# Storing the cache gradients of a decode step's backward pass from ScalarE, one head later, with the last two heads in parts

## The chip, the cores and the metric

The kernel runs on one core of a Trainium2 chip. The metric is the device time of one launch in microseconds, taken as the median of several runs. Times inside the kernel come from one profiled execution.

## The reference

The reference computes one decode step of a transformer layer (batch 4, one token each, D = 512, 32 heads of 128, a key and a value cache of 4096 positions per head) and its gradients for a given `grad_out`, all in bf16:

```
xn = layernorm(x);  q = xn @ wq                       # per batch b and head h: q of 128
p  = softmax(q . K^T / sqrt(128));  o = p @ V         # K, V: [4, 32, 4096, 128]
h  = x + concat(o) @ wo
h2 = h + (silu(hn @ w1) * (hn @ w3)) @ w2,  hn = layernorm(h)
outputs: h2, and the gradients of x, k_cache, v_cache, wq, wo, w1, w3, w2
```

The large part is the caches. There are 4 x 32 = 128 heads, and each has 1 MB of keys and 1 MB of values. For one head with output gradient dO (128 values) the backward pass is

```
dP = V @ dO                     # 4096 values
dS = p * (dP - c) * scale       # c = dO . o
grad of V = p  (outer) dO       # 4096 x 128, out_3
grad of K = dS (outer) q        # 4096 x 128, out_2
```

So keys and values are read once for the forward pass (256 MB), the values are read a second time for dP (128 MB), and 256 MB of outer products are written.

## The kernel before, in words

The order of all work is written out by hand; every engine executes its instructions in program order. All large tiles live in 22 equal buffers in SBUF, called slots. A slot is taken from the front of one queue (`free`) and given back at its end (`give`), at the place in the program where the last use is written; the next user of the slot waits for that last use, for instance until a store from it has landed.

The forward part (until about 690 us of the trace) loads K and V head by head on SP's DMA queue and computes the softmax and, per head, a 128 x 128 product. A middle part (690 to 720 us) does the gated unit and its gradients. The backward loop over the 128 heads `s` then follows, from 720 us on; `b, h = s % B, s // B`. In one iteration:

- `prefetch(s + 1)` issues loads of V on SP's queue, up to seven heads ahead and as long as more than five slots are free.
- `front(s + 1)` transposes that head's V on TensorE in four groups of eight blocks (L739), ScalarE copies each group from PSUM to the slot VT (L740), TensorE multiplies VT by dO (L1070, dP), and GpSimd writes the pairs of p (L1073). Every fourth head, `replicate` makes the broadcast rows `rq` and `rdo` (L1054 on TensorE, L1057 on ScalarE).
- `back(s)` makes the two outer products on VectorE (both at L1077): first gv, the gradient of V, then dS (L1092, L1095), then gk, the gradient of K. After each of them GpSimd issued the store of the 1 MB (L1089, L1099), and the slot was given back there.
- `step("s", n)` lets `n` pieces of the side work run: the gradients of x, wq, wo, w1, w3, w2, which use TensorE, ScalarE and slots of their own, and whose stores GpSimd issues (gwq, gw, gwo). It runs one piece per head for 44 heads and then two, with a third on every fourth head.

After the loop the rest of the side work would run; in this kernel it has ended by then.

At the start of the loop most slots are taken: eight by the forward products (Ms, given back during the first 48 heads), ten by loaded V, one by `rs`.

Of the kernel before, what the change touches and what calls it, by code (L numbers as in the profile page):

```python
# [24 lines left out]
def kernel(  # L25
# [22 lines left out]
    nc = tc.nc  # L48
    P = nc.NUM_PARTITIONS

    B = A_x.shape[0]
    D = A_x.shape[-1]
    H = A_k_cache.shape[1]
# [30 lines left out]
    def bh_of(s):  # L84
        return s % B, s // B

    def rows_of(ap):
        return ap.rearrange("(p j) d -> p j d", p=P)
# [83 lines left out]
    def ones_window(col):  # L172
# [11 lines left out]
                          in_=rowg[:, None, :, None].to_broadcast([P, 4, 8, 4]))  # L184
# [414 lines left out]
    def step(k, n=1):  # L599
        for _ in range(n):  # L600
            next(units[k], None)
# [131 lines left out]
    def V_T(s, ps):  # L733
        VTs[s] = Slot("VT")
        VT, Vn = VTs[s].heads(), V2s[s].heads()
        for g in range(SJ // GW):
            pt = ps.tile([P, GW, P], BF16, tag="tps", name="pt_tps")
            for i in range(GW):
                nc.tensor.transpose(pt[:, i, :], Vn[:, g * GW + i, :], ident_b[:])  # L739
            nc.scalar.copy(out=VT[:, g * GW:(g + 1) * GW, :], in_=pt[:])  # L740
        V2s.pop(s).give()
# [3 lines left out]
    def load_V2():  # L745
        s = nv["next"]
        if s < NH:
            V2s[s] = Slot("V2")
            nc.sync.dma_start(out=V2s[s].heads(), in_=cache_head(A_v_cache, s))
            nv["next"] += 1  # L750
# [125 lines left out]
    with ExitStack() as c2:  # L876
# [173 lines left out]
        def replicate(i0):  # L1050
            for nm_, rows in (("rdo", dOrows_bf), ("rq", qrows_bf)):
                ps = psrep.tile([P, REP, Dh], FP32, tag="rep", name="rep_ps")
                for i in range(REP):
                    nc.tensor.matmul(ps[:, i, :], lhsT=ident_b[:, i0 + i:i0 + i + 1].to_broadcast([P, P]), rhs=rows[:],  # L1054
                                     start=True, stop=True)
                rt = rep_bufs[nm_][i0 // REP % 2]
                nc.scalar.copy(out=rt, in_=ps[:])  # L1057
                reps[nm_, i0 // REP] = rt
# [3 lines left out]
        def front(s):  # L1062
            if s % REP == 0:
                replicate(s)
            if s not in VTs:
                V_T(s, psT)
            VT = VTs[s].heads()
            dP_ps = psD.tile([P, SJ], FP32, name="dP_ps", tag="dP")
            for j in range(SJ):
                nc.tensor.matmul(dP_ps[:, j:j + 1], lhsT=VT[:, j, :], rhs=dOT_bf[:, s:s + 1], start=True, stop=True)  # L1070
            VTs.pop(s).give()
            P2 = bw3.tile([P, SJ, 2], BF16, tag="P2", name="P2")
            nc.gpsimd.tensor_copy(out=P2[:], in_=P_all[:, s, :, None].to_broadcast([P, SJ, 2]))  # L1073
            bwd[s] = (dP_ps, P2)

        def outer(dst, col2, row):
            nc.vector.tensor_tensor(  # L1077
                out=dst.rearrange("p j (r t) -> p j r t", t=2),
                in0=col2[:, :, None, :].to_broadcast([P, SJ, Dh // 2, 2]),
                in1=row.rearrange("p (r t) -> p r t", t=2)[:, None, :, :].to_broadcast([P, SJ, Dh // 2, 2]),  # L1080
                op=ALU.mult,
            )

        def back(s):
            b, h = bh_of(s)
            dP_ps, P2 = bwd.pop(s)
            gv = Slot("gv")
            outer(gv.heads(), P2, reps["rdo", s // REP][:, s % REP, :])
            nc.gpsimd.dma_start(out=rows_of(out_3[b, h]), in_=gv.heads())  # L1089
            gv.give()  # L1090
            t = bw3.tile([P, SJ], FP32, tag="dSt", name="dSt")
            nc.vector.tensor_scalar(out=t[:], in0=dP_ps[:], scalar1=c_rep[:, s:s + 1], scalar2=scale,  # L1092
                                    op0=ALU.subtract, op1=ALU.mult)
            dS2 = bw3.tile([P, SJ, 2], BF16, tag="dS2", name="dS2")
            nc.vector.tensor_tensor(out=dS2[:], in0=t[:, :, None].to_broadcast([P, SJ, 2]),  # L1095
                                    in1=P_all[:, s, :, None].to_broadcast([P, SJ, 2]), op=ALU.mult)
            gk = Slot("gk")
            outer(gk.heads(), dS2, reps["rq", s // REP][:, s % REP, :])
            nc.gpsimd.dma_start(out=rows_of(out_2[b, h]), in_=gk.heads())  # L1099
            gk.give()  # L1100

        def prefetch(s):
            while nv["next"] < min(NH, s + 7) and len(free) > 5:
                load_V2()

        prefetch(0)
        front(0)
        for s in range(NH):
            prefetch(s + 1)
            if s + 1 < NH:  # L1110
                if s + 1 not in V2s and s + 1 not in VTs:
                    load_V2()
                front(s + 1)
            back(s)
            step("s", 1 if s < 44 else 2 + (s % 4 == 0))
        step("s", 400)


# [28 lines left out]
```

## Time and profile before

| what | value |
|---|---|
| median of 8 runs | 1742.61 us (1740.53 to 1749.5) |
| the profiled execution | 1749.5 us, span 1747.7 us |
| DMA | 707.86 MB, mean 405 GB/s |
| busy share | PE 75%, DVE 72%, ACT 55%, POOL 28% |
| one outer product on VectorE | 2.29 us, 256 of them |
| one copy of eight transposed blocks on ScalarE | 1.015 us, 512 of them |
| issue of one store on GpSimd | 0.53 us, 256 of them; median to landing 20 us |
| first and last store of the loop | issued at 722.0 and 1727.5 us |

In the lines of the profile PE is TensorE (PEld its weight loads), DVE is VectorE, ACT is ScalarE, POOL is GpSimd and SP is SyncE, whose queue issues the loads. `out<-in` names the tile that an instruction writes and the one that it reads. A row of waits reads: engine, its instruction, what it waited for; total us, how often, longest. A row of windows gives the busy time and the number of instructions of each engine, then the granted TensorE clock, the mean busy share of the 16 DMA engines, and their rate in GB/s.

### The profile page before, as it was taken

To read this page: it belongs to the slowest core of one execution; us is meant where nothing else is said; L and a number is where in the kernel's file an instruction comes from. 1 tells how busy PE (TensorE), PEld (TensorE's weight loads), DVE (VectorE), ACT (ScalarE), POOL (GpSimd) and SP (SyncE) were. 2 spreads that over 40 slices of the span, in tenths; PEclk is the share of its full clock that TensorE was granted. 3 is DMA by queue.
4 is the path that set the end of the run, shared out by engine and by line. 5 is a ranking of instruction groups with operands and counts; after the bars stand their busy time and mean duration, and the time that the engine had idled before them with its cause. 6 is when DMAs were issued, how large, how long until landed. Compare 5 with 4: busy or idle time off the path is not lost.

```text
span 1747.7 us, 44065 instructions
## 1 busy us (share of the span) xinstructions
PE 1316.4 (75%) x18993; PEld 1112.7 (64%) x18993; DVE 1251.6 (72%) x1382; ACT 955.6 (55%) x1463; POOL 483.4 (28%) x804
## 2 busy tenths in 40 slices
PE   5889888888888888888777876676667657786653
PEld 4777776666666667877767875565445545564543
DVE  5899899899898996567756866648545546665665
ACT  3455445445444444656555665575556656676643
POOL 2333333333333330122322421212212112222232
PEclk8999999999999999655555557676556655556565
DMA  9999999999999999799999999999999999999997
GB/s 398 410 418 418 419 418 419 419 416 418 413 417 394 418 404 359 304 421 411 418 419 419 415 418 414 420 423 375 422 383 405 411 400 411 391 411 415 405 421 313
DMA packets 107123, 707.86 MB, mean 405 GB/s; under 512 B 11232, under 2 KB 18920, under 8 KB 23984
## 3 DMA queue, kind: packets, MB, share of 16 engines
q1 hardware_dynamic: 67280, 422.68, 59.4%
q0 software_dynamic: 39648, 282.36, 39.2%
q8 instruction: 149, 2.44, 0.5%
q14 instruction: 46, 0.38, 0.1%
HBM read 422.58 MB, written 282.34 MB: 403 GB/s over the span
## 4 chain that ended last, share of the span: by engine, by line
DMA 32%; PE 9%; DVE 9%; ACT 7%; issue 6%; POOL 1%; DVEq 0%; POOLq 0%; ACTq 0%
DMA out_dram<-gk 21%; DMA out_dram<-gv 8%; ACT VT L740 6%; DVE gk L1077 4%; PE pt_tps L739 3%; DVE gv L1077 3%; DMA out_dram<-gwo 2%; PE dq_ps L902 2%; DMA out_dram<-gw 1%; PE dP_ps L1070 1%; PE M_ps L436 1%; DVE PK L421 1%; PE pt_wo L573 1%; POOL P L1073 0%; PE rep_ps L1054 0%
## 5 line engine op out<-in xcount | busy, mean ns | idle before, releaser
L740 ACT COPY VT<-pt_tps 128x1024 bf16<-128x1024 bf16 x512 | 492.7, 1015 | 292.2 <-PE pt_tps L739 141.9
L739 PE MATMUL pt_tps<-ident_b,V 128*128 128x128 bf16 x4096 | 446.5, 291 | 179.0 <-ACT VT L740 171.3
L739 PEld LDWEIGHTS <-V 128*128 128x128 bf16 x4096 | 396.7, 137 | 246.4 <-issue 228.6
L1077 DVE TENSOR_TENSOR gv<-P,reps 128x4096 bf16<-128x4096 bf16 x128 | 292.9, 2288 | 254.2 <-DMA out_dram<-gk 145.1
L1077 DVE TENSOR_TENSOR gk<-dS,reps 128x4096 bf16<-128x4096 bf16 x128 | 293.4, 2292 | 79.0 <-DMA out_dram<-gk 32.6
L421 DVE TENSOR_TENSOR PK<-Kn,PK 128x4096 bf16<-128x4096 bf16 x128 | 302.8, 2366 | 37.3 <-POOL PK L417 37.3
L436 PE MATMUL M_ps<-PK,Vn 128*128 128x130 bf16 x4096 | 287.5, 223 | 53.7 <-DMA Vn<-in_A_v_cache_dram 53.6
L436 PEld LDWEIGHTS <-Vn 128*128 128x128 bf16 x4096 | 254.3, 99 | 74.3 <-DMA Vn<-in_A_v_cache_dram 66.9
L328 DVE STREAM_TRANSPOSE KT<-Kn 128x512 f32<-128x512 f32 (+1 forms) x321 | 250.8, 798 | 0.5 <-issue 0.5
L323 ACT COPY KT<-pt_tps 128x1024 bf16<-128x1024 bf16 x128 | 129.4, 1012 | 194.1 <-PE pt_tps L322 161.4
L1070 PE MATMUL dP_ps<-dOT_bf,VT 128*128 128x1 bf16 x4096 | 152.7, 166 | 75.8 <-ACT VT L740 64.4
L1070 PEld LDWEIGHTS <-VT 128*128 128x128 bf16 x4096 | 140.8, 104 | 89.0 <-ACT VT L740 76.9
L1099 POOL DMA_DIRECT2D out_dram<-gk x128 | 68.2, 532 | 392.3 <-DVE gk L1077 376.5
L1089 POOL DMA_DIRECT2D out_dram<-gv x128 | 68.5, 535 | 354.3 <-DVE dSt L1092 337.4
L417 POOL COPY PK<-P_all 128x64 bf16<-128x64 bf16 x128 | 32.3, 252 | 437.7 <-ACT P_all L411 432.5
L336 POOL COPY zq<-qT_bf 128x2 bf16<-128x2 bf16 x128 | 152.2, 1189 | 0.0
L1073 POOL COPY P<-P_all 128x64 bf16<-128x64 bf16 x128 | 114.1, 892 | 0.0
L411 ACT COPY P_all<-pt_P 32x64 bf16<-32x64 bf16 x256 | 51.9, 203 | 59.7 <-PE pt_P L407 57.4
L322 PE MATMUL pt_tps<-ident_b,Kn 128*128 128x128 bf16 x1024 | 80.0, 222 | 0.7 <-DVE qrep L282 0.7
L446 PE MATMUL kP_ps<-PK,onesw 128*32 128x512 bf16 x1024 | 80.1, 390 | 0.0
L322 PEld LDWEIGHTS <-Kn 128*128 128x128 bf16 x1024 | 61.6, 99 | 26.3 <-issue 26.2
L400 ACT ACTIVATE Pn<-E,rl 128x1024 bf16<-128x1024 f32 x64 | 73.7, 1152 | 2.8 <-DVE rl L397 2.8
(234 smaller groups left out, 1301.2 us busy)
## 6 DMA issues: line engine op xcount, KB each, us to landing
Kn<-in_A_k_cache_dram SPq DMA_DIRECT2D x128, 1024.0 KB, 14.8
Vn<-in_A_v_cache_dram SPq DMA_DIRECT2D x128, 1024.0 KB, 15.5
V<-in_A_v_cache_dram SPq DMA_DIRECT2D x128, 1024.0 KB, 11.7
out_dram<-gv POOLq DMA_DIRECT2D x128, 1024.0 KB, 20.1
out_dram<-gk POOLq DMA_DIRECT2D x128, 1024.0 KB, 20.3
wq<-in_A_wq_dram SPq DMA_DIRECT2D x8, 1024.0 KB, 11.2
out_dram<-gw POOLq DMA_DIRECT2D x6, 896.0 KB, 21.6
wo<-in_A_wo_dram SPq DMA_DIRECT2D x4, 1024.0 KB, 11.7
```

Source lines behind the costliest of these rows:

```text
L322: nc.tensor.transpose(pt[:, i, :], Kn[:, c * GW + i, :], ident_b[:])
L323: nc.scalar.copy(out=KT[:, c * GW:(c + 1) * GW, :], in_=pt[:])
L328: nc.vector.transpose(out=KT[:, c * w_:(c + n) * w_], in_=Kn[:, c * w_:(c + n) * w_])
L336: nc.gpsimd.tensor_copy(out=zq[gi % 2][hl][:, 32:132:67], in_=qT_bf[:, s:s + 1].to_broadcast([P, 2]))
L421: nc.vector.tensor_tensor(out=PK[:, :, 0:Dh].rearrange("p j (r t) -> p j r t", t=2), in0=Ks[s].heads().rearrange("p j (r t) -> p j r t", t=2),
L436: nc.tensor.matmul(hold["M"][:], lhsT=Vn[:, j, :], rhs=PK[:, j, :], start=(j == 0), stop=(j == SJ - 1))
L446: nc.tensor.matmul(hold["kP"][32 * q:32 * (q + 1), :, :], lhsT=ones_window(w), rhs=PK[:, j0:j0 + 4, 0:Dh], start=(w == 0 and c == 0), stop ...
L739: nc.tensor.transpose(pt[:, i, :], Vn[:, g * GW + i, :], ident_b[:])
L740: nc.scalar.copy(out=VT[:, g * GW:(g + 1) * GW, :], in_=pt[:])
L1070: nc.tensor.matmul(dP_ps[:, j:j + 1], lhsT=VT[:, j, :], rhs=dOT_bf[:, s:s + 1], start=True, stop=True)
L1073: nc.gpsimd.tensor_copy(out=P2[:], in_=P_all[:, s, :, None].to_broadcast([P, SJ, 2]))
L1077: nc.vector.tensor_tensor(out=dst.rearrange("p j (r t) -> p j r t", t=2), in0=col2[:, :, None, :].to_broadcast([P, SJ, Dh // 2, 2]), in1=r ...
```

## The change

The stores of a head are taken out of `back(s)`. `back` appends the two slots to a queue `late`, and a new function `store_late(eng)` issues the two stores of the oldest entry on the engine that it is given and gives the slots back. In the loop it is called with ScalarE between `front(s + 1)` and `back(s)`, so the stores of head s stand in ScalarE's queue after the copies of head s + 2. Heads 0 and 1 are stored by GpSimd right after their `back`. For the last head of the two last batches (h = 31, b = 2 and 3, which are s = 126 and 127) each store is cut into one of 120 partitions and one of 8. The last entry is stored after the loop, before the rest of the side work. The side work gets its third piece on every third head instead of every fourth. The side work's own stores stay on GpSimd.

```
 def back(s):
     ...
     outer(gv.heads(), P2, reps["rdo", s // REP][:, s % REP, :])
-    nc.gpsimd.dma_start(out=rows_of(out_3[b, h]), in_=gv.heads())
-    gv.give()
     ...
     outer(gk.heads(), dS2, reps["rq", s // REP][:, s % REP, :])
-    nc.gpsimd.dma_start(out=rows_of(out_2[b, h]), in_=gk.heads())
-    gk.give()
+    late.append((b, h, gv, gk))
+
+late = deque()
+
+def store_late(eng):
+    b, h, gv, gk = late.popleft()
+    for out_ap, sl in ((out_3, gv), (out_2, gk)):
+        cut = [0, 120, P] if h == H - 1 and b >= B - 2 else [0, P]
+        for p0, p1 in zip(cut[:-1], cut[1:]):
+            eng.dma_start(out=rows_of(out_ap[b, h])[p0:p1], in_=sl.heads()[p0:p1])
+        sl.give()
 ...
+S0 = 0
 prefetch(0)
 front(0)
 for s in range(NH):
     ...
         front(s + 1)
+    if late:
+        store_late(nc.scalar)
     back(s)
-    step("s", 1 if s < 44 else 2 + (s % 4 == 0))
+    if s < 2:
+        store_late(nc.gpsimd)
+    if s >= S0:
+        step("s", 1 if s < S0 + 44 else 2 + (s % 3 == 0))
+store_late(nc.scalar)
 step("s", 400)
```

## The prediction

> **What bounds the kernel now.** I read the 40 slices first, then the queues and the issues, then the stages by window, then the waits, and last the timeline of both ends of the backward part.
>
> ```profile
> DMA  9999999999999999799999999999999999999997
> GB/s 398 410 418 418 419 418 419 419 416 418 413 417 394 418 404 359 304 421 411 418 419 419 415 418 414 420 423 375 422 383 405 411 400 411 391 411 415 405 421 313
> q1 hardware_dynamic: 67280, 422.68, 59.4%
> q0 software_dynamic: 39648, 282.36, 39.2%
> V<-in_A_v_cache_dram SPq DMA_DIRECT2D x128, 1024.0 KB, 11.7
> out_dram<-gv POOLq DMA_DIRECT2D x128, 1024.0 KB, 20.1
> out_dram<-gk POOLq DMA_DIRECT2D x128, 1024.0 KB, 20.3
> ```
>
> The 16 DMA engines are busy in every slice but the middle one (17) and the last. 707.86 MB are moved and the change moves no byte more or less, so it can only change idle DMA time, the speed of a packet, and what follows the last byte. A V load lands in 11.7 us, a store in 20: stores queue.
>
> ```profile
> core 0: us, PE busy (x) PEld busy (x) DVE busy (x) ACT busy (x) POOL busy (x), PEclk, DMA share, GB/s
> 720.00:740.00 20.00, 16.98 (x224) 15.91 (x223) 14.33 (x12) 13.53 (x15) 5.17 (x9) 0.59 0.63 233
> 740.00:752.00 12.00, 10.03 (x135) 9.33 (x134) 5.64 (x5) 7.19 (x9) 1.40 (x4) 0.62 1.00 394
> 752.00:1180.00 428.00, 326.93 (x4116) 298.54 (x4114) 275.96 (x227) 249.76 (x272) 113.26 (x166) 0.59 1.01 418
> 1180.00:1660.00 480.00, 324.71 (x3960) 258.46 (x3956) 289.10 (x241) 299.37 (x375) 116.00 (x187) 0.59 0.99 403
> 1732.00:1736.00 4.00, 0.00 (x0) 0.00 (x0) 0.00 (x0) 0.00 (x0) 0.00 (x0) 0.50 0.87 367
> 1736.00:1740.00 4.00, 0.00 (x0) 0.00 (x0) 0.00 (x0) 0.00 (x0) 0.00 (x0) 0.50 0.21 90
> 1740.00:1744.00 4.00, 0.00 (x0) 0.00 (x0) 0.00 (x0) 0.00 (x0) 0.00 (x0) 0.50 0.06 25
> ```
>
> The last two columns matter. The backward loop starts with a DMA that is not full (0.63), is full from 740 on, loses rate after 1180 (403 against 418), and ends with a tail in which few engines still write: a share of 0.06 is one engine of 16. ScalarE is busy 250 of 428 us and 299 of 480: it has room for more issues.
>
> ```profile
> DVE gv L1077 <- DMA out_dram<-gk: 145.1, 37, 9.8
> ACT VT L740 <- DMA out_dram<-gv: 49.2, 12, 8.8
> ACT VT L740 <- DMA out_dram<-gk: 48.8, 11, 11.6
> ```
>
> The waits of the backward loop say the same: the products and the V^T copies wait until a store has landed and its slot is free.
>
> **One finding behind the page.** A transfer's semaphore counts 16 engines. In the trace's semaphore events the 16th engine of a store comes 0.4 us after the 15th between 740 and 900 us (median), 6.5 us after it between 1200 and 1650, 3.1 us after it for the very last store (1740.8, then 1743.9); for loads before 660 us it is 0.1 us. Packets follow one another on an engine within 3 to 4 ns, so the packet records can be put into 16 chains: between 1700 and 1716 eight or nine chains write 8 KB in 309 ns each, without exception, and four or five take 314 to 321 ns on the mean. So some engines are slower than the rest, only while GpSimd's queue is in use, and a slot waits for the slowest. On one point the measured queue numbers are no help: packets of both queues cost the same (39.2% for 282 MB, 59.4% for 423 MB).
>
> **The change, part by part.** The profiled execution took 1749.5 us (1.8 around its span of 1747.7); the median of the runs is 1742.6. The terms below are differences and I put them on the median. 0.2%, about what a measurement of this kernel can tell from no change, is 3.5 us: 1739.1 to 1746.1.
>
> *Who issues.* 252 stores of 1 MB leave GpSimd (0.53 us each, idle there anyway) for ScalarE. The trace has no ScalarE store. The nearest rows are SP's loads: 0.33 us alone, 1.1 to 1.6 us each when several follow one another in the backward loop. Two per head make 0.7 to 3 us; between two heads ScalarE idles 1.34 to 2.6 us for TensorE's first eight transposes (timeline), which is the cover. Taken at +1 us in all, 0 to +8.
>
> *Slow engines.* If the slow chains come from GpSimd's way of issuing, they go. Time of 8 KB packets over 309 ns is 2.05% of the engines in 740 to 1180 (9 us) and 3.4% in 1180 to 1660 (16 us); together 25 us at most. At the other end the packets of SP's queue in the load-only stage took 316.6 ns on the mean against 315.8 for the stores in 900 to 1150, so it could cost 2.5 us over the 1000 us of the loop. I take -16, about two thirds, as the chains differ by engine, which mixing reads and writes would not explain, and as the lag of the 16th engine is absent where only the hardware queue works.
>
> [...]
>
> *One head later.* The pair of head s now leaves after front(s+2), behind the four V^T copies in ScalarE's queue; queued behind the store's wait for DVE's gk are the side work's copies and those of the next head, for which TensorE waits. In the full stretch DMA has a 20 us queue and this costs nothing. It does where there is no queue. At the start: heads 0 and 1 go as before (GpSimd, 722.0 to 734.4). Head 2 left at 736.6 and 739.3; now it leaves when front(4) ends, at 750.7 (copies at 746.66 and 748.77, 1.93 each), and front(4) waits for TensorE, not for stores, so it is no earlier. The load of V 10 goes from 736.2 to 741.3: two slots held back mean that it takes the slot of V 3. So 740 to 752, now 394 GB/s x 12 = 4.7 MB, would move that 1 MB: 3.7 MB at 418 are 8.8 us of DMA time that nothing gives back, as DMA is full until 1728. Bounds +5 (part of the next loads come earlier) to +12.
>
> *Slots.* Counted in program order the loads of V still run seven heads ahead and 8 to 12 slots stay free where 10 to 14 did; the side work ends at head 114 instead of 116 (s % 3). Each is covered by the full DMA queue: 0; without that cover it is the slower rival below.
>
> *The tail.* Head 124 now leaves at 1718.6 and 125 and 126 at 1723.9 (end of front(127)), where they left from 1709 to 1722. A store takes 2.45 us of all engines (8 rows x 306 ns). Pair 124 then ends at about 1725, six more stores at 1739.5; an evenly shared tail would have ended at 1737.1 (0.21 x 4 + 0.06 x 4 = 1.1 us of work after 1736). That is +2.5; 0 to +5, as loads that overtake stores bring the last fronts forward.
>
> *120 and 8 partitions.* No row shows such a store. 128 rows are 8 on each engine; if 120 go to 15 engines and 8 to eight of them, four stores spare one engine 32 rows = 9.9 us and load eight others with 4 rows = 1.2 us. If the spared engine is the late one, the end comes from the 15th, 1740.8 instead of 1743.9: -3. If not, 0 to +1.2. I take -3 with -5 to +1.
>
> *End of the program.* GpSimd's final drain starts at 1727.5 and lasts 19.4 us, to 1746.9; SP was through at 1744.5. With its last store long landed, GpSimd is ready before SP: -2.3, sure.
>
> Sum: +1 - 16 + 8.8 + 2.5 - 3 - 2.3 = -9.0; 1742.6 - 9.0 = 1733.6, say 1734.
>
> **The rivals.** *Slower:* the slow packets come from reads and writes mixed, not from the issuer, and the late pair starves DMA again in the loop. Place: ScalarE's V^T copies that wait for a slot (the two rows above, 98 us in 23 waits, up to 11.6); finished products now stand behind them, and GpSimd used to send them meanwhile. At 1290 the DMA share already fell to 0.3 to 0.55 for 4 us in such a wait. A tenth to a fifth of the 98 us lost is +10 to +20. With +8.8 + 2.5 + 1 - 2.3 - 3 that is 1760 at most, 1752 likely when the engines even out in part. It decides as soon as the gain on slow engines is under 3.5 us, or the starving exceeds it. For it: front(s+1) waits for the pair of s-3, so ScalarE's queue closes a loop. Against: two more pairs are then in flight, 10 us of work, against 6 us of copies.
>
> *No change:* the engines gain 5 to 9 us and the early gap takes it: 1739 to 1746. *Not as said:* the spared engine is not the late one; that moves any case by 3 us and is within the ranges.
>
> **How the numbers follow.** Engines even out by half or more: 0.50, 1723 to 1739, likeliest 1734. No change: 0.15. Slower: 0.35, 1746 to 1762. The range 1723 to 1757 leaves out the far ends of the first and the last. Chances: faster 0.50, same 0.15, slower 0.35.
>
> **What would show it.** In the profile after: 1180:1660 near 415 GB/s and the 16th engine within 1 us of the 15th (the -16 right); a hole of 8 to 9 us in the DMA share between 740 and 752 (the early gap right); after the last store's landing less than 2 us to the end (the drain right); the share before the end falling from 0.9 to 0 within 4 us (the split right). Wrong if the store stages stay at 403 to 418 GB/s, or if new waits of ScalarE for DVE's gk come with DMA shares below 0.9.

## The result, and the profile after

The changed kernel takes 1756.83 us (median; 1754.56 to 1757.87); the kernel before, beside it on the same chips, 1743.35 us. The ratio is 1.0071, 95% interval 1.0056 to 1.0085: 12.4 us slower (the plain difference of the two medians is 13.5). The profiled execution took 1757.8 us with a span of 1756.0. The forecast was 1734 with a range of 1723 to 1757: the sign was wrong, and 1756.8 lies in the range only by its upper edge. One thing is to be kept in mind with every comparison of profiles below: the profiled execution of before (1749.5 us) was 6 us slower than the median of that kernel, while those of the changed kernel and of the others lie within 2 us of theirs, except e1 (4 us under) and e15 (8 us under).

The rate of the 40 slices, the queues and the issues of the page after:

```profile
GB/s 397 410 418 418 419 418 419 418 414 419 415 416 400 415 410 360 260 384 414 421 418 414 422 421 411 389 385 416 425 424 415 400 409 409 412 412 412 420 402 264
q1 hardware_dynamic: 67280, 422.68, 59.3%
q10 hardware_dynamic: 36316, 264.26, 36.4%
q0 software_dynamic: 3360, 18.11, 2.5%
out_dram<-gv ACTq DMA_DIRECT2D x124, 1024.0 KB, 13.2
out_dram<-gk ACTq DMA_DIRECT2D x124, 1024.0 KB, 14.8
```

The 264 MB of stores have moved from the software queue q0 to a hardware queue, q10. Slice 17 is emptier (260 GB/s, before 304), and so is the last (264 against 313). A store now lands in 13 to 15 us, where it took 20.

The stages by window (the last two columns are the mean DMA share and GB/s):

```profile
720.00:740.00 20.00, 17.27 (x243) 16.09 (x240) 14.91 (x12) 13.65 (x15) 6.68 (x9) 0.59 0.52 212
740.00:752.00 12.00, 9.50 (x114) 8.78 (x115) 7.06 (x7) 6.99 (x9) 0.24 (x1) 0.64 0.59 220
752.00:1180.00 428.00, 309.29 (x3966) 283.48 (x3964) 270.69 (x221) 237.52 (x259) 12.75 (x54) 0.60 1.00 409
1180.00:1660.00 480.00, 338.79 (x3994) 266.33 (x3995) 285.06 (x239) 305.50 (x382) 37.14 (x71) 0.60 1.01 414
...
1728.00:1732.00 4.00, 0.00 (x0) 0.00 (x0) 0.07 (x1) 0.00 (x0) 0.00 (x0) 0.50 0.96 315
1732.00:1736.00 4.00, 0.00 (x0) 0.00 (x0) 0.00 (x0) 0.00 (x0) 0.00 (x0) 0.50 0.89 307
1736.00:1740.00 4.00, 0.00 (x0) 0.00 (x0) 0.00 (x0) 0.00 (x0) 0.00 (x0) 0.50 0.90 260
1740.00:1744.00 4.00, 0.00 (x0) 0.00 (x0) 0.00 (x0) 0.00 (x0) 0.00 (x0) 0.50 0.60 160
1744.00:1748.00 4.00, 0.00 (x0) 0.00 (x0) 0.00 (x0) 0.00 (x0) 0.00 (x0) 0.50 0.59 184
1748.00:1752.00 4.00, 0.00 (x0) 0.00 (x0) 0.00 (x0) 0.00 (x0) 0.00 (x0) 0.50 0.06 27
```

Against the rows of before: 740 to 752 fell from 394 to 220 GB/s, 752 to 1180 from 418 to 409, and 1180 to 1660 rose from 403 to 414. At the end the engines are 0.89 to 0.96 busy from 1728 to 1740 and yet move only 260 to 315 GB/s; in the loop a share of 0.96 goes with 368 (1120 to 1140, below) and one of 1.00 with 409. So packets are slow there: the 8 KB packets that start after 1728 take 416 ns on the mean in the packet records, a quarter of them 500 or more, where 90% of those from 740 to 1660 take 309.

Summed from the packet records and put into us at 420 GB/s, the kernel after stands 1.0 us behind before at 740, 7.4 at 760, 7.0 at 1100, 14.2 at 1180, 1.3 at 1660 and 3.5 at 1728. So it had won back much of what it lost when the products ended (1728.07, before 1727.2), and 7.6 us more were lost after that: the last store landed at 1755.0, before at 1743.9, 11.1 us later.

The same sums warn against the two large windows. What the changed kernel loses between 1100 and 1180 (7.0 to 14.2 us) it has back at 1300 (5.7), because the kernel before has its own slow spells just behind the edge at 1180. After, at 1120, and before, at 1180 and 1280:

```profile
1120.00:1140.00 20.00, 14.88 (x216) 12.37 (x215) 8.32 (x8) 14.26 (x16) 0.24 (x1) 0.76 0.96 368
```

```profile
1180.00:1200.00 20.00, 9.40 (x123) 6.86 (x120) 14.84 (x19) 6.37 (x8) 4.62 (x8) 0.74 0.91 368
1280.00:1300.00 20.00, 8.96 (x85) 6.42 (x84) 14.63 (x12) 6.02 (x9) 4.38 (x8) 0.50 0.90 343
```

Most of "409 for 418" and "414 for 403" is therefore one slow spell in each kernel, which falls before the edge in one and behind it in the other, and not a slower and a faster stage.

The waits for stores became shorter:

```profile
DVE gv L1077 <- DMA out_dram<-gk: 102.8, 22, 13.6
ACT VT L740 <- DMA out_dram<-gv: 28.0, 7, 5.8
ACT VT L740 <- DMA out_dram<-gk: 14.4, 4, 6.5
```

The V^T copies now wait 42 us for stores instead of 98. The timeline of ScalarE's queue at the end shows the issues of the parts (start, duration, two issues in each row):

```profile
1724.64 3.60 ACTq L1110 DMA_DIRECT2D out_dram<-gv  x2
1728.34 4.11 ACTq L1110 DMA_DIRECT2D out_dram<-gk  x2
1732.54 6.59 ACTq L1110 DMA_DIRECT2D out_dram<-gv  x2
1739.22 4.48 ACTq L1110 DMA_DIRECT2D out_dram<-gk  x2
```

The issues themselves stand: one of them takes up to 3.6 us, and the last of the eight ends at 1743.7, 16 us after the products.

ScalarE's queue stands in front of stores in the loop, too. Here the product gv of a head ended at 1141.7 and ScalarE's copies at 1143.1, and the store left 6.3 us after that:

```profile
1141.19 1.93 ACT L740 COPY VT<-pt_tps 128x1024 bf16<-128x1024 bf16 x2 [0.18 <-PE pt_tps L739]
1149.42 0.34 ACTq L1110 DMA_DIRECT2D out_dram<-gv  x1
```

The semaphores (counters) that the instructions name in the trace say why. The landings of SP's loads and ScalarE's stores are counted on the same eight semaphores in turn (83 or 84 transfers on each), and a store whose queue stands waits there on its own semaphore, for an earlier transfer. In the trace of after this happens 58 times for 0.2 us or more, 152.7 us in all, 8.5 at most; for 44 of them a landing on that semaphore stands within 0.3 us before the issue, for the other 14 the counts can't be put to single transfers. In the kernel before GpSimd's stores had eight semaphores of their own, and none of its 264 stores of the loop left within 0.3 us of such a landing.

### The profile page after: what moved, and what is told of

Same layout as the page of the kernel before. It is cut to its first block, busy times and chain, and to the rows that moved or that the text cites. A ratio compares the mean times of both kernels' runs of the same rounds, so it can differ in the third digit from the quotient of the medians.

```text
span 1756.0 us, 43821 instructions
## 1 busy us (share of the span) xinstructions
PE 1319.0 (75%) x18993; PEld 1108.8 (63%) x18993; DVE 1252.7 (71%) x1382; ACT 957.0 (54%) x1463; POOL 282.3 (16%) x552
## 4 chain that ended last, share of the span: by engine, by line
DMA 35%; PE 10%; ACT 9%; DVE 5%; issue 2%; ACTq 1%; POOL 0%; SPq 0%; DVEq 0%
DMA out_dram<-gk 14%; DMA out_dram<-gv 10%; DMA V<-in_A_v_cache_dram 8%; ACT VT L740 7%; PE pt_tps L739 4%; DVE gv L1077 2%; DVE gk L1077 1%; DMA wq<-in_A_wq_dram 1%; DMA out_dram<-gwo 1%; ACTq L1110 1%; PE rep_ps L1054 1%; PE dq_ps L902 1%; DMA out_dram<-gwq 1%; DMA w2a<-in_B_w_dram 1%; PE dP_ps L1070 1%
## 5 line engine op out<-in xcount | busy, mean ns | idle before, releaser
L1073 POOL COPY P<-P_all 128x64 bf16<-128x64 bf16 x128 | 46.7, 380 | 592.7 <-DVE gv L1077 592.7
L1090 DVE TENSOR_SCALAR dSt<-dP_ps,c_rep 128x32 f32<-128x32 f32 x128 | 31.6, 247 | 91.7 <-PE dP_ps L1070 91.7
L1057 ACT CAST reps<-rep_ps 128x512 bf16<-128x512 f32 x64 | 37.5, 585 | 69.6 <-PE rep_ps L1054 55.9
## 6 DMA issues: line engine op xcount, KB each, us to landing
out_dram<-gk ACTq DMA_DIRECT2D x124, 1024.0 KB, 14.8
```

## The experiments

Each kernel is given with its ratio to the kernel before on the same chip, and the 95% interval. e1 to e4 ran beside a before of 1743.83 us, e5 to e8 of 1744.83, e9 to e11 of 1745.09, e12 to e14 of 1746.08, e15 and e16 of 1743.90.

**e1, whole stores at the end.** From the change:

```
-cut = [0, 120, P] if h == H - 1 and b >= B - 2 else [0, P]
+cut = [0, P]
```

> The changed kernel with the last two heads stored whole again (no parts of 120 and 8 partitions). Theory A (the parts jam ScalarE's queue: its last ten issues took 1.0 to 3.6 us each and the last one left 16 us after its data were ready): 1747 to 1750 us, 7 to 10 less than the change. Rival B (the end is set by one slow engine that the parts give four rows more, 1.2 us): 1755 to 1756. In the trace A expects the issues after 1724 us under 1 us each and the last landing near 1746; B expects the last landing near 1754.

1748.72 us, 1.0029 [1.0013, 1.0044]. Without the parts 0.42% (7.3 us) come back. The windows of its end and the timeline of ScalarE's queue:

```profile
1728.00:1732.00 4.00, 0.00 (x0) 0.00 (x0) 0.00 (x0) 0.00 (x0) 0.00 (x0) 0.50 1.02 426
1732.00:1736.00 4.00, 0.00 (x0) 0.00 (x0) 0.00 (x0) 0.00 (x0) 0.00 (x0) 0.50 0.53 223
1736.00:1740.00 4.00, 0.00 (x0) 0.00 (x0) 0.00 (x0) 0.00 (x0) 0.00 (x0) 0.50 0.12 49
```

```profile
1721.63 1.15 ACTq L1110 DMA_DIRECT2D out_dram<-gv  x1
1722.87 1.17 ACTq L1110 DMA_DIRECT2D out_dram<-gk  x1
```

A share of 1.02 is 426 GB/s again (8 KB packets of 311 ns), and a whole store is issued in 1.2 us.

**e2, parts of 112 and 16.** `[0, 112, P]` instead of `[0, 120, P]`.

> The changed kernel with parts of 112 and 16 partitions instead of 120 and 8: as many transfers, but each part can go to all 16 engines evenly. If the number of transfers behind each other jams the queue (A), it stays at 1754 to 1757. If the uneven sharing out is what costs (B, one engine spared, eight with nine rows), it falls to the time with whole stores.

1754.89 us, 1.0061 [1.0041, 1.0081], and packets of 391 ns after 1728. In the semaphore events each part of 112 and of 16 has 16 counts that come with data, so the rows are shared out evenly, and it did not help: the interval overlaps that of the change, and uneven shares are not what costs.

**e3, heads 0 to 9 stored at once by GpSimd.** `s < 10` instead of `s < 2`; the parts stay.

> The changed kernel with heads 0 to 9 stored by GpSimd at once instead of heads 0 and 1; the first late store then comes when the DMA has a queue. The running sum of bytes is 7.4 us behind at 760 us. Theory C (that time is lost for good, DMA being full afterwards): 1748 to 1751 us, 6 to 8 less than the change. Rival D (the loop is bound by something else too and makes it up by 1660 us, as the sum is only 1.3 us behind there): 1755 to 1757.

1748.37 us, 1.0021 [1.0007, 1.0036]: 0.5% (8.7 us) faster than the change. The hole is gone, as the window shows, and in the sum of bytes this kernel stands 0.2 us behind before at 760 and at 1100, where the change stands 7.4 and 7.0:

```profile
740.00:752.00 12.00, 10.00 (x134) 9.29 (x132) 5.29 (x5) 7.28 (x9) 1.46 (x4) 0.62 1.00 389
```

**e4, all stores late, whole, and on GpSimd.** `store_late(nc.gpsimd)` throughout, no parts.

> One part alone: the stores one head late and whole, with the side work's new pace, but all issued by GpSimd. If lateness alone costs (early gap, fewer stores in the queue at the end): 1747 to 1751 us. If the issuing by ScalarE costs (its queue, its slow issues): 1742 to 1745, as before the change. If GpSimd's issues slow some engines, the lag of the 16th engine should be 6 us and more in 1200 to 1650 us here, as before.

1737.86 us, 0.9968 [0.9953, 0.9983]: neither expectation, faster than before. On GpSimd the late place is not late, since nothing stands in its queue in front of the store but the copy of p (L1073); the hole hardly opens (360 GB/s from 740 to 752). What remains of the change is that slots are given back later in the program and the side work's pace. The 16th engine lags here as in before: 8.7 us behind the 15th at 1200 to 1500 (median of the semaphore events), 9.2 at 1500 to 1650. Yet 1180 to 1660 moves 413 GB/s:

```profile
752.00:1180.00 428.00, 327.09 (x4158) 296.98 (x4155) 280.52 (x232) 250.53 (x273) 112.64 (x171) 0.61 1.01 418
1180.00:1660.00 480.00, 337.67 (x3945) 270.26 (x3944) 285.03 (x239) 299.70 (x375) 119.28 (x183) 0.54 1.01 413
```

So the rate of that stage does not hang on the lag.

**e5, before with the new pace alone** (`s % 3` for `s % 4`), and **e6, e4 with the old pace.**

> The kernel before with one edit of the change alone: a third piece of side work on every third head instead of every fourth. Theory E (the better rate after 1180 us, 413 to 416 GB/s in every kernel with that pace against 403, comes from the pace): 1736 to 1740 us. Rival F (it comes from the slots, which are given back one head later): 1742 to 1745, as before.

> The kernel with all stores written one head late, whole, and issued by GpSimd, but at the old pace of the side work (every fourth head). E: 1742 to 1745 us. F: 1736 to 1740. If both parts matter: in between, 1740 to 1742.

e5: 1740.28 us, 0.9970 [0.9950, 0.9990]; e6: 1740.59 us, 0.9969 [0.9950, 0.9988]. Each alone gives 0.3%, and both together (e4) give 0.3% too: they reach the same gain. Neither E nor F says that; e6 lies where "both parts matter" was expected, e5 0.3 us above E's range. The stage rates of e5:

```profile
752.00:1180.00 428.00, 327.01 (x4167) 297.65 (x4165) 278.52 (x228) 250.68 (x273) 112.46 (x168) 0.60 1.01 419
1180.00:1660.00 480.00, 332.83 (x3926) 265.94 (x3926) 292.27 (x246) 297.58 (x373) 125.37 (x188) 0.55 1.00 410
```

**e7, ScalarE without the two costs:** whole stores as in e1 and ten early heads as in e3.

> The changed kernel without the parts and with heads 0 to 9 on GpSimd, both costs undone together. If the gap at the start and the jam at the end are two costs that add (8.1 and 8.5 us): 1739 to 1742 us, near the same stores on GpSimd (1737.9). If undoing one already undoes the other, or ScalarE's issues cost elsewhere: 1745 to 1749.

1739.63 us, 0.9958 [0.9940, 0.9976]. With e1, e3 and the change it makes a table of two by two:

| | early hole | no hole (`s < 10`) |
|---|---|---|
| parts at the end | 1.0071 | 1.0021 (e3) |
| whole stores | 1.0029 (e1) | 0.9958 (e7) |

The hole costs 0.50 to 0.71%, 8.7 to 12.4 us, the parts 0.42 to 0.63%, 7.3 to 11.0 us, and both together 1.13%, 19.7 us. Whether they add exactly can't be read from ratios with intervals of 0.15% and more on either side (e7 was measured beside other runs of before than the rest); the medians alone give 8.5 or 9.1 for the hole, 8.1 or 8.7 for the parts and 17.2 for both, which is the sum. Without them the change is a gain of 7.3 us, and e7 beats the kernel before, as e4, e5 and e6 do; among these four the intervals decide nothing. The windows of e7:

```profile
740.00:752.00 12.00, 9.63 (x115) 8.90 (x116) 4.87 (x5) 7.09 (x9) 1.30 (x3) 0.64 1.01 423
752.00:1180.00 428.00, 320.05 (x4018) 291.17 (x4016) 278.43 (x228) 242.19 (x265) 21.28 (x70) 0.60 1.00 408
1180.00:1660.00 480.00, 335.23 (x3997) 264.60 (x3996) 284.32 (x238) 303.50 (x379) 42.21 (x70) 0.59 1.01 414
```

Against e4, which differs in who issues and in the heads that leave at once: 408 against 418 GB/s before 1180 and the same after. The loss isn't spread over the stage: by the sum of bytes e7 is 0.6 us ahead of e4 at 1100 and 8.4 behind at 1180; in two windows of 20 us from 1120 on it moves 341 and 362 GB/s, e4 424 and 425. In that spell ScalarE's queue stands 6.2 and 5.6 us in front of a store (at 1107 and 1143) on its own semaphore; in the whole loop it does so 56 times, 156 us in all. That these stands make the spell is likely, but no run takes them away alone. e7 is still 7.0 us behind e4 at 1728; e4 in turn ends with a longer lag and GpSimd's last drain, and the medians come out alike.

**e8, the parts of the last two heads issued by SP.**

```
-                store_late(nc.scalar)
+                store_late(nc.sync if s == NH - 1 else nc.scalar)
...
-        store_late(nc.scalar)
+        store_late(nc.sync)
```

> The changed kernel with the parts of 120 and 8 partitions of the last two heads issued by SP, whose queue is empty by then. Theory A1 (the parts wait because ScalarE's queue is full of stores that one late engine has not done): issues of 0.3 to 0.5 us, 1746 to 1750 us. Rival A2 (transfers of 120 and 8 partitions are slow to issue by themselves, on any queue): issues stay at 1 to 3 us, 1753 to 1757 us.

1752.97 us, 1.0035 [1.0014, 1.0057]: between the change and e1, whose interval it overlaps, so it doesn't say how much of the cost ScalarE's queue makes. It does say that this is not all: the eight issues still take 0.3 to 3.0 us each on a queue that had no loads left, and 8 KB packets after 1728 still take 392 ns on the mean. That speaks for A2, though the time lies just under its range. The test isn't clean either. SP's parts and ScalarE's stores share eight semaphores, and ScalarE's two stores of head 125 left only when an earlier transfer on theirs had landed, at 1728.1 and 1730.0 (in the change at 1723.6 and 1724.0); three of SP's last four issues followed on such a landing too.

**e9 and e10, cuts in the middle of the loop.** From e7, the 16 heads s = 64 to 79 alone; by partitions (e9) and by columns (e10):

```
-cut = [0, P]
+cut = [0, 120, P] if 16 <= h < 20 else [0, P]            # e9

+cut = [0, SJ // 2, SJ] if 16 <= h < 20 else [0, SJ]      # e10: [:, j0:j1]
```

> The kernel of e7 (heads 0 to 9 on GpSimd at once, all stores whole), but the 16 heads s = 64 to 79, in the middle of the loop, are stored in parts of 120 and 8 partitions. Theory P (transfers of 120 or 8 partitions are slow by themselves: their 8 KB packets took 350 to 520 ns in the tails of the change, e2 and e8 against 311 for whole stores): 32 stores x 2.45 us x 0.2 to 0.4 = 16 to 31 us more than e7, 1755 to 1770 us, with packets of 370 ns or more in the stage where these heads are stored. Rival Q (only a short queue at the end makes parts costly): 1738 to 1742 us, packets as in e7.

> The same 16 heads in two transfers each as in e9, but each of all 128 partitions and half of the columns (4 KB rows). Theory P (the partition count is what costs): 1738 to 1743 us, as e7. Rival N (the number of transfers or of issues costs): about as e9, 1755 us or more if e9 is.

e9: 1790.24 us, 1.0259 [1.0233, 1.0285]; e10: 1754.25 us, 1.0048 [1.0025, 1.0070]. Against e7 that is 50.6 us for 32 stores, 1.6 us each, and 14.6 us, 0.5 us each. Cutting by partitions is what costs most, as P says, but both times lie outside P's ranges: the price of e9 is above its upper bound, and a transfer more costs something too, which neither theory had at that size.

**e12, e13 and e14.** e12 and e13 store 8 partitions a second time behind each whole store, `[120:P]` or `[0:P:16]`; e14 is e9 with `[0, 64, P]`.

> The kernel of e7 (all stores whole), but for the 16 heads s = 64 to 79 each whole store is followed by a second one of its last 8 partitions (120 to 127) with the same data: 32 transfers of 64 KB, 2.1 MB or 5 us of DMA time more. Theory H (eight engines that read eight neighbouring partitions, or write eight neighbouring rows, at the same time get in each other's way): most of what e9 cost above e7 (50.6 us) comes back, 1765 to 1785 us, with 8 KB packets of 360 ns or more from 1240 to 1420. Rival N (a transfer more costs as in e10): e7 + 5 + up to 15, 1745 to 1760 us. Rival U (the 15 engines of the part of 120 are what costs): e7 + 5, 1745 us.

> As e12, but the second store takes 8 partitions spread over the tile (0, 16, 32, ... 112): as many transfers, bytes and engines as e12. Theory H (neighbouring partitions): 1745 to 1750 us, the 5 us of bytes and little else, packets near 315 ns. Rival N (the number of transfers, or their small size): as e12, within 4 us.

> The kernel of e9 with the 16 heads stored in two parts of 64 partitions: four rows for each of the 16 engines, shared out evenly. Theory H: two engines share each eight neighbouring partitions, so something, but far less than e9: 1742 to 1758 us. Rival U (uneven sharing over 15 and 8 engines is what costs): no more than e10, 1740 to 1754 us. Rival A (any transfer that is not of all 128 partitions is slow): as e9, 1780 to 1795 us.

e12: 1889.91 us, 1.0818 [1.0758, 1.0877]; e13: 1884.69 us, 1.0793 [1.0745, 1.0841]. These two don't answer the question: the second store writes the same rows of DRAM, and in the trace its issue waits until the first has landed. ScalarE's queue in e12:

```profile
1297.39 0.34 ACTq L1108 DMA_DIRECT2D out_dram<-gv  x1
1305.28 0.30 ACTq L1110 DMA_DIRECT2D out_dram<-gv  x1
```

The store of 1297.39 lands at 1305.2, and only then does the small one leave. They do give a price: a queue of ScalarE that stands 4 to 8 us for each of 32 stores makes the kernel about 4.5 us longer for each ((1884.69 - 1739.63) / 32). e14: 1789.71 us, 1.0245 [1.0203, 1.0287]. Halves cost as much as 120 and 8, which is A's time; e16 below speaks against A's reason.

**e15, e9 with the parts issued by GpSimd; e16, e14 with the even and the odd partitions as the two parts.**

```
+store_late(nc.gpsimd if 64 <= s - 1 < 80 else nc.scalar)            # e15
+cut = [(0, 2), (1, 2)] if 16 <= h < 20 else [(0, 1)]                # e16: [p0:P:st]
```

> The kernel of e9, with the parts of 120 and 8 partitions of the 16 heads issued by GpSimd instead of ScalarE, at the same place in the program. Theory I (ScalarE stands in its issues: 59 us of issue time from 1240 to 1430 against 22 in e7, and every product behind it waits): most of the 50 us goes, 1740 to 1755 us. Rival D (the transfers themselves are slow): 1775 to 1790 us, with 8 KB packets of 370 ns or more from 1240 to 1420, as in e9.

> The kernel of e14, but the two parts of 64 are the even and the odd partitions instead of the lower and the upper half: if the rows are shared out in order, four to an engine, each engine now keeps to the same group of eight partitions as in a whole store. Theory M (the cost comes from engines that leave their group and meet another engine there): as e10, 1745 to 1758 us, mean 8 KB packets under 340 ns. Rival A (any transfer of fewer than 128 partitions is slow): as e14, 1785 to 1795 us, packets of 390 ns.

e15: 1770.42 us, 1.0145 [1.0097, 1.0194]; e16: 1765.31 us, 1.0112 [1.0069, 1.0155]. Both times fall between their theories (e16's packets, 339 ns, are as M said): part of the cost is ScalarE's issue time, part is slow transfers, and these depend on which partitions a part has. The window that holds these heads, in e7, e9, e10, e14, e15 and e16 in this order:

```profile
1240.00:1430.00 190.00, 138.74 (x1621) 108.21 (x1621) 118.50 (x98) 123.89 (x154) 18.84 (x29) 0.60 1.01 414
1240.00:1430.00 190.00, 105.41 (x1161) 79.92 (x1161) 88.47 (x71) 89.76 (x112) 8.89 (x21) 0.56 0.85 295
1240.00:1430.00 190.00, 130.85 (x1490) 100.57 (x1490) 110.09 (x89) 115.01 (x143) 14.55 (x25) 0.62 0.99 377
1240.00:1430.00 190.00, 105.02 (x1158) 80.70 (x1157) 88.02 (x71) 89.41 (x112) 9.53 (x21) 0.56 0.90 298
1240.00:1430.00 190.00, 114.81 (x1413) 90.62 (x1413) 101.92 (x85) 106.65 (x132) 52.07 (x82) 0.63 0.97 355
1240.00:1430.00 190.00, 122.00 (x1417) 95.54 (x1415) 105.43 (x86) 108.47 (x136) 14.41 (x25) 0.60 0.92 355
```

Two things are to be read in the last two columns: the share falls (engines wait, 0.85 in e9, 0.97 when GpSimd issues), and a given share moves less (slow packets). The packet and issue records of a stretch of 32 products around these heads take both apart:

| | stretch, us | share | mean 8 KB packet, ns | of the stores | of V's loads | issue time on ScalarE, us |
|---|---|---|---|---|---|---|
| e7 whole | 122.4 | 1.01 | 314 | 312 | 317 | 15.7 |
| e9 120 and 8 | 179.8 | 0.84 | 376 | 376 | 380 | 56.1 |
| e14 lower and upper half | 178.1 | 0.90 | 398 | 404 | 394 | 67.0 |
| e15 120 and 8, GpSimd issues | 144.7 | 0.95 | 359 | 370 | 335 | 0 |
| e16 even and odd | 151.8 | 0.91 | 339 | 313 | 391 | 39.1 |
| e10 halves of the columns | 143.1 | 0.98 | 371 (mostly V loads) | 164 (4 KB; elsewhere 159) | 390 | 35.9 |

The two columns by queue tell more than the mean. The packets of the stores are slow where a part is a run of neighbouring partitions (376, 404 and 370 ns against 312), and not where it is every second partition (313) or half of the columns. So 64 partitions in place of 128 do not by themselves make a store's packets slow (313 ns in e16), and A is wrong. The packets of V's loads are slow in all four kernels in which ScalarE issues cut stores (380 to 394), the columns included, and less so where GpSimd issues them (335); no run tells why.

**e11, e4 with the last head's two stores on SP.**

> The kernel of e4 (all stores whole and late, from GpSimd), but the last head's two stores are issued by SP. If GpSimd's last drain (19.4 us from its last issue in the kernel before) ends the program, it now ends with SP: 2.3 us less than e4, 1735 to 1736 us, and the span ends within 1.2 us of the last landing. Rival (the drain hides behind the last landing): 1738 us, as e4.

1738.81 us, 0.9964 [0.9948, 0.9981]: as e4, and the question stays open, because GpSimd's stores still landed last. SP's two stores, issued at 1710.7 and 1713.5, landed at 1721.1 and 1725.7 on all 16 engines; GpSimd's, issued from 1702.5 to 1710.4, had their last engine 6.4 to 11.5 us after the 15th, and the last of them landed at 1734.3. The span still ended 3.7 us after that last landing.

## Why the prediction was wrong, by its steps

*120 and 8 partitions*: -3 was forecast, with +1 as the worst; it is +7.3 to +11.0. It failed, and by 10 to 14 us, but it doesn't turn the sign alone: e1, without the parts, is still 0.29% slower than before. The missing 16 us of the next step do the rest. The sharing was right: in the semaphore events a part of 120 shows one early count and 15 that come with data, a part of 8 one and eight. The engine that it spares is not the late one: in the gv of head 126 the other engines of the 120 were done by 1736.5 and the late one at 1746.4, and it took part in the store of 8 too (1746.7). That was named as "not as said", at 3 us. What was not weighed at all is that packets of such a part are slow (416 ns in this tail) and that its issue stands up to 3.6 us. The traces of after, e2, e9, e14 and e15 show the slow store packets, those of after, e8, e9 and e14 the long issues, and e1 shows that both go with the parts.

Why these packets are slow no run shows; in the trace of after a quarter of those after 1728 take 500 ns or more. What the runs tell apart is the choice of the part: the stores' packets take 404 ns for the lower and the upper half (e14) and 313 for even and odd partitions (e16), and the halves of the columns leave e10's 4 KB packets near their 159 ns (164).

*Slow engines*: -16 was forecast, and this is the largest step that failed. In the prediction's own measure, the time of 8 KB packets over 309 ns, the profiles give 9.0 us in 740 to 1180 and 16.2 in 1180 to 1660 before, 13.3 and 11.2 after: 25.2 and 24.4 in all, a gain of 0.8 us. e7 has 24.5, e4 (GpSimd) 21.9, and the times of e4 and e7 are alike. The mistake was to take the late engine for the cost. The lag did shrink: in 1200 to 1650 the 16th engine comes 2.5 to 3.9 us after the 15th (median) in the six kernels whose loop is stored whole by ScalarE (after, e1, e2, e3, e7, e8; the longest is 6.4 at 1500 to 1650 in after, before 5.3), 5.5 to 9.4 in the five with GpSimd (before, e4, e5, e6, e11). Between 900 and 1180 it is 0.2 to 0.6 against 1.9 to 3.6. So the issuer, or the number of stores on its queue, does bear on the lag. What remains of it after 1180 may still come from GpSimd, which issues the 14 stores of the side work between 1232 and 1647; no run takes these away. But the lag doesn't set the rate: e4 has one of the largest and moves 413 GB/s, after moves 414. A term of 0 would have been near the 0.8 us that were measured. The forecast sign for 1180 to 1660 came true (414, forecast 415) for other reasons, which makes it luck: the pace, next, and a profile of before that lies 6 us over its median.

*Slots* and the pace: taken at 0; e5, e6 and e4 give -5 us each by their ratios, and in the profiles nearly all of it lies in 1180 to 1660 (403 to 410, 412 and 413). These rates overstate it, as 403 belongs to an execution 6 us over the median. "Covered by the full DMA queue" was the mistake: in that stage the queue of before was not always full, as the shares of 0.91 and 0.90 at 1180 and 1280 show.

*Who issues*: +1 was forecast, 0 to +8. All ScalarE's issues of after make 139 us (median 339 ns each), and 152.7 us more go in the stands in front of them, for which the prediction had no term. Against e4, e7 is 7.0 us of bytes behind at 1728, and yet their times are alike (0.9968 and 0.9958); no run separates this step from the rest of what the two differ in. The slower rival's place, finished products behind V^T copies that wait for slots, did not show: those waits fell to 42 us. Finished products did wait in ScalarE's queue, but at the stores themselves, for the landing of an earlier transfer. The rival's time (1746 to 1762) came true without its reason. Its sum was off as well: 1742.6 + 7.0 + 10 to 20 is 1760 to 1770 and not 1760 at most.

*One head later*: +8.8 was forecast; e3 and e7 give 8.7 to 12.4, and the bytes are 7.4 us behind at 760. Right, place and size. *The tail*: +2.5 was forecast; no run takes it alone, and the 3.5 us of bytes behind at 1728 hold the rest of the hole too, so it stays open. *End of the program*: -2.3 forecast; from the last landing to the end of the span 3.7 us before and 1.0 after, -2.7. Right.

The sum by the runs: -7.3 for all that e7 keeps (forecast -14.8 with the tail), +19.7 for the hole and the parts (forecast +5.8), which is +12.4. The pace and the slots (-5) and the end of the program (-2.7) already make up the -7.3, so the sum leaves nothing for the issuer, though small gains and losses may hide in it. Of the signs that the prediction named, the hole and the end of the program came, and so did 414 GB/s, though without the 16th engine catching up; the share before the end fell over some 20 us instead of 4.

Open: why the late engine is late, what the stands at shared semaphores cost, why V's loads slow down beside cut stores, and how the 50.6 us of e9 divide exactly between issue time and slow packets (e15 puts 20 us of it on ScalarE's queue).

## What to carry to other kernels

In this kernel, whose DMA share is 1.00 and 1.01 in the two large windows after, a store of a whole 128-partition tile was cheaper than each of the pairs of transfers tried (1.6 us more for runs of partitions, 0.8 for even and odd, 0.5 for halves of the columns). If a tile must be cut, try the columns first, and measure what the transfer more costs. "Covered by the full DMA queue" did not hold here in the stage that moved 403 GB/s against 418, where the pace alone was worth 0.30% (e5): compare the GB/s of each window first, and move the edges of the windows before a difference is believed. A lag was no loss here (413 GB/s with 8.7 us in e4): sum the time that packets take over their best before a late engine is priced. When stores change their queue, look which semaphores they share from then on (here ScalarE's queue stood 152.7 us on such ones, after). When stores go behind another engine's work in its queue, look for the stage where the DMA is not full: here the lateness of one head stayed there (220 GB/s from 740 to 752, 8.7 to 12.4 us).

## What the runs showed of the hardware that I had not expected

- Two transfers of 64 partitions cost 1.6 us more than one of 128 (e14), and the stores' 8 KB packets went from 312 to 404 ns; even and odd partitions leave them at 313 (e16), two of half the columns cost 0.5 us more (e10).
- The issue of a store on ScalarE took 0.34 us at the median in after and at most 1.6 before 1700, but up to 3.6 while stores in parts were under way; SP's issues of parts took up to 3.0 (e8). Whole stores at the end of e1 took 1.15 to 1.4. No run shows what a long issue waits for.
- In e11 the lag of one engine stayed with GpSimd's stores: SP's second store, issued at 1713.5 after four of GpSimd's, was complete on all 16 engines at 1725.7, while three of these were still short of one.
- The lag of the 16th engine cost no rate in the full stages: 413 GB/s with 8.7 us (e4), 414 with 2.8 to 6.4 (after).
- Stores on ScalarE's queue stood 58 times on the semaphore that they share with SP's loads and with each other, 152.7 us in all (after); of GpSimd's 264 stores in before and in e4, on eight semaphores of their own, none did.
